# Sliding-window attention, then a dropless mixture of experts, in one program: a pair's gate weights a portion later, the third pair's tasks packed, row stores from SyncE, another order of the first loads, and the index table in two parts

## The chip, the cores and the metric

The kernel runs on one core of one Trainium2 chip. The metric is the device time of one execution, in microseconds; less is better. The core has five engines that run side by side and wait for one another by semaphores: PE (TensorE, matrix products and transposes), DVE (VectorE), ACT (ScalarE), POOL (GpSimd) and SP (SyncE, which here only issues DMA transfers). Each engine works through its own instructions in the order in which the program has them. SP, ACT and POOL issue DMA transfers.

## The reference

```python
# attention: q, k, v are (8, 8, 576, 64): batch, heads, positions, head size
scores = q @ k^T / sqrt(64) + slope[h] * -(|i - j|)     # slope[h] = 2 ** -(h + 1)
scores = where((i - j >= 0) & (i - j < 128), scores, -1e9)
attn   = softmax(scores);  x = attn @ v                 # x as 4608 tokens of 512

# experts: w_gate 512 x 8, w1 8 x 512 x 1024, w2 8 x 1024 x 512
logits = x @ w_gate
e      = argmax(logits);  gate_w = softmax(logits)[e]
y      = relu(x @ w1[e]) @ w2[e]                        # for every token its own expert
out    = gate_w * y
```

Each token goes to one expert, and no token is dropped.

## The kernel before

**Attention.** Two batches make a pair (`bp`, 0 to 3), two heads make a head pair (`hp`, 0 to 3). One pair and one head pair are a unit `u` of 16, and each unit has four portions, so that a counter `i` runs from 0 to 63. Portion `i` does `scores(i + 2)` (PE products into a PSUM tile `sp`, of which there are two; ACT's exponential into `pe`; DVE's multiplication of `pe` by the distance factors `fac`) and then `values` of its own (PE products of `v_sb` and `pe` into a PSUM tile `at`, of which there is one). In the third and fourth portion of a unit, `finish` has ACT copy `at` to `xT` in SBUF, has PE add up the softmax sums in a PSUM tile `m`, and has DVE put these into `sumT`. Because there is one `at`, the second half of a unit can't begin before ACT has copied the first. There are two `m` tiles, shared by all the helpers below.

**A pair's tasks.** When a pair's four units are through, `behind(bp)` queues its routing as a list of portions' worth of work, one entry at the end of each following portion. For each pair: `gate` (PE: logits before scaling; DVE adds the sums), `turn` (PE transposes, ACT copies), `scale_a` and `scale_b` (DVE: divides by the softmax sums, finds the best expert `sel`, and, with ACT's exponential of `ex` in between, the gate weight, which goes to `ext`), `count` (DVE: running counts `pre`), `place` (PE adds the counts of earlier tokens, DVE makes slot numbers), `ones_at` and `enlist` (the token numbers are put into the table `listed` by a product of one-hot matrices), and nine times `row` (PE transposes 128 tokens, ACT copies them to `xs`, POOL adds `ext`, and a DMA writes them to `x_rows` in memory). The fourth pair's tasks lie in the first expert's products (`with_tail`).

**Experts.** `fixed[e]` is a group of 512 tokens of expert e, worked by a Strassen scheme: `strassen1` (first layer) and `strassen2` (second), each of 14 steps of eight matmul rows, with one entry of the list `fill` behind each step. Seven `further` groups of 128 take what is over. A group's tokens come by `gather` (POOL: indirect DMA from `x_rows` by the index table `g_idx`), are scaled by DVE (`to_scale`, tile `xn`), and turned by PE (`to_columns`, tile `xgT`). Expert 0 is taken from the first three pairs alone, so that its `gather` (index by `early_table`) needs only their rows. The indices of all other groups come from `tables`, after `count_all`.

The order of the work on each engine is that of the code: nothing is rearranged by a scheduler (`manual_schedule`).

## Time and profile before

| | us |
|---|---|
| median of three runs | 753.37 (751.31 to 754.02) |
| the profiled execution | 751.79 |
| its span, first to last instruction | 749.8 |
| PE busy | 690.3 (92%) |
| DVE busy | 348.2 (46%) |
| ACT busy | 223.3 (30%) |
| POOL busy | 157.7 (21%) |

Spans and starts are read from the first instruction of the profiled execution. The profiled execution is 2.0 us longer than its span. PE's granted clock is given as a share of full speed: 1.00 is 2.4 GHz and 0.50 is 1.2 GHz; the mean over the span is 0.97. Matmuls are pipelined in the trace, so the start of the next group tells more than the end of one.

### The profile page before, as it was taken

What the parts mean: (1) busy time and instruction counts of PE and PEld (TensorE: products, weight loads), DVE (VectorE), ACT (ScalarE), POOL (GpSimd) and SP (SyncE); (2) the same over time, 40 slices, a digit from 0 to 9 for tenths busy, and PEclk for the clock granted to TensorE, in tenths of its full rate; (3) what the DMA queues carried; (4) which work ended last, traced back from release to release, by engine and by line L of the source; (5) the groups of instructions that cost most, each with busy time, mean ns of one, the idle gap of its engine ahead of it and who ended that gap; (6) DMA issues with size and microseconds to landing.
All of it is one profiled execution on the core that took longest, in us unless ns stands there. A gap on an engine that the chain in (4) does not pass through costs nothing.

```text
span 749.8 us, 14527 instructions
## 1 busy us (share of the span) xinstructions
PE 690.3 (92%) x6204; PEld 574.7 (77%) x6204; DVE 348.2 (46%) x649; ACT 223.3 (30%) x402; POOL 157.7 (21%) x258
## 2 busy tenths in 40 slices
PE   4997986996869979999999999999999999999993
PEld 3876865765748868887888888788788978878891
DVE  2556557557435926551545254254435435433410
ACT  3643553553424312321320231132023123203210
POOL 4310430521502415012102302200230230021020
PEclk9998998998979989999999999999999999999997
DMA  9876674760341746318336732822763382184010
GB/s 255 252 216 218 191 233 123 226 193 30 122 153 72 278 176 231 112 42 295 142 113 205 271 112 73 305 100 109 245 232 113 107 307 90 81 279 143 1 58 7
DMA packets 49756, 122.00 MB, mean 163 GB/s; under 512 B 3648, under 2 KB 14496, under 8 KB 49681
## 3 DMA queue, kind: packets, MB, share of 16 engines
q1 hardware_dynamic: 37856, 85.92, 33.8%
q0 software_dynamic: 10688, 34.16, 13.5%
q8 instruction: 51, 0.84, 0.5%
q10 hardware_dynamic: 1136, 0.88, 0.4%
q14 instruction: 25, 0.20, 0.1%
HBM read 101.79 MB, written 19.96 MB: 162 GB/s over the span
## 4 chain that ended last, share of the span: by engine, by line
issue 53%; POOL 10%; PE 7%; DMA 3%; DVE 1%; ACT 1%; POOLq 0%; ACTq 0%; DVEq 0%
POOL out_dram L1329 5%; POOL xg L1071 5%; DMA xg<-x_rows,g_idx 2%; DMA x_rows<-xs 2%; PE pair0a L1249 1%; PE pair0b L1249 1%; PE m L976 1%; PE m L1088 1%; PE at L767 0%; PE pair2b L1249 0%; PE pair2a L1249 0%; PE pair0a L1306 0%; ACT xs L978 0%; PE m L819 0%; PE m L964 0%
## 5 line engine op out<-in xcount | busy, mean ns | idle before, releaser
L1329 POOL DMA_INDIRECT out_dram<-zo,s_idx x39 | 44.1, 1130 | 385.9 <-DVE zo L1320 284.7
L767 PE MATMUL at<-pe,v_sb 64*64 64x192 f32 (+2 forms) x1408 | 64.7, 301 | 25.2 <-ACT xT L784 20.8
L741 DVE TENSOR_TENSOR pe<-pe,fac 128x768 f32<-128x768 f32 x48 | 46.0, 958 | 61.7 <-ACT pe L738 61.7
L767 PEld LDWEIGHTS at<-pe,v_sb 64*64 64x64 f32 x1408 | 50.0, 144 | 31.8 <-ACT xT L784 23.2
L738 ACT ACTIVATE pe<-sp 128x768 f32<-128x768 f32 x64 | 51.8, 809 | 50.8 <-PE sp L732 49.3
L732 PE MATMUL sp<-q_sb,k_sb 64*64 64x192 f32 (+2 forms) x1152 | 62.0, 335 | 5.3 <-DMA q_sb<-in_qT_dram 5.3
L732 PEld LDWEIGHTS sp<-q_sb,k_sb 64*64 64x64 f32 x1152 | 42.8, 143 | 18.6 <-issue 6.0
L1071 POOL DMA_INDIRECT xg<-x_rows,g_idx x39 | 42.9, 1101 | 22.6 <-issue 11.3
L1089 ACT COPY xgT<-m 128x512 f32<-128x512 f32 x39 | 22.8, 585 | 49.9 <-PE m L1088 49.0
L1088 PE MATMUL m<-ident,xn 128*128 128x128 f32 x156 | 25.8, 292 | 11.4 <-DVE xn L501 11.4
L501 DVE TENSOR_TENSOR xn<-xg 128x512 f32<-128x512 f32 x39 | 26.3, 687 | 21.3 <-DMA xg<-x_rows,g_idx 13.3
L1088 PEld LDWEIGHTS m<-ident,xn 128*128 128x128 f32 x156 | 20.7, 151 | 16.4 <-issue 11.9
L1260 ACT ACTIVATE h<-h 128x512 f32<-128x512 f32 x32 | 20.2, 631 | 36.9 <-DVE h L1259 36.9
L799 PE MATMUL m<-pe,ind 128*32 128x192 f32 (+2 forms) x704 | 31.0, 296 | 0.0
L978 ACT COPY xs<-m 128x512 f32<-128x512 f32 x36 | 20.7, 584 | 33.4 <-PE m L976 23.5
L981 POOL DMA_DIRECT2D x_rows<-xs x40 | 22.2, 556 | 35.9 <-ACT xs L978 19.9
L607 POOL DMA_DIRECT2D v_sb<-in_v_dram x15 | 11.5, 769 | 84.3 <-PE at L767 84.2
L799 PEld LDWEIGHTS m<-pe,ind 128*32 128x32 f32 x704 | 24.3, 114 | 2.7 <-issue 0.4
L979 POOL COPY xs<-ext 128x16 f32<-128x16 f32 x36 | 16.7, 464 | 39.5 <-DVE ext L900 37.7
L976 PE MATMUL m<-ident,xT 128*128 128x128 f32 x144 | 22.7, 286 | 2.4 <-DVE sumT L810 1.0
L746 DVE TENSOR_TENSOR pe<-pe,fac 128x768 f32<-128x768 f32 x16 | 17.4, 1090 | 13.7 <-ACT pe L738 13.7
L976 PEld LDWEIGHTS m<-ident,xT 128*128 128x128 f32 x144 | 16.1, 145 | 7.5 <-issue 2.2
(353 smaller groups left out, 1412.1 us busy)
## 6 DMA issues: line engine op xcount, KB each, us to landing
w<-in_moe_w_dram SPq DMA_DIRECT2D x30, 2048.0 KB, 10.9
k_sb<-in_kT_dram SPq DMA_DIRECT2D x15, 576.0 KB, 5.0
q_sb<-in_qT_dram SPq DMA_DIRECT2D x15, 576.0 KB, 6.3
x_rows<-xs POOLq DMA_DIRECT2D x32, 264.0 KB, 2.5
v_sb<-in_v_dram SPq DMA_DIRECT2D x16, 288.0 KB, 4.0
v_sb<-in_v_dram POOLq DMA_DIRECT2D x15, 288.0 KB, 5.0
x_rows<-xs POOLq DMA_DIRECT2D x8, 132.0 KB, 3.1
xg<-x_rows,g_idx POOLq DMA_INDIRECT x39, 6.6
```

Source lines behind the costliest of these rows:

```text
L501: nc.vector.tensor_tensor(to.rearrange("p (h d) -> p h d", h=H), rows[:, :Dm].rearrange("p (h d) -> p h d", h=H), rows[:, Dm : Dm + H].uns ...
L732: nc.tensor.matmul(sp[c * KB : (c + 1) * KB, r, c0 : c0 + n], lhsT=k_sb[u][hs, c, kb * KB : (kb + 1) * KB], rhs=q_sb[u][hs, c, kb * KB : k ...
L738: nc.scalar.activation(pe[:], sp[:, :, :GC], AF.Exp, scale=SCALE)
L741: nc.vector.tensor_tensor(pe.rearrange("p r (k c) -> p r k c", k=2), pe.rearrange("p r (k c) -> p r k c", k=2), fac[:, h0 : h0 + 2, None, ...
L767: nc.tensor.matmul(acc[r * D : (r + 1) * D, c, lo - q0 : hi - q0], lhsT=v_sb[u][c * KB : (c + 1) * KB, kb, r * D : (r + 1) * D], rhs=pe[c ...
L799: nc.tensor.matmul(sm[32 * j : 32 * j + 32, lo - q0 : hi - q0], lhsT=none[:] if pe is None else ind[:, hp, :], rhs=fac[:, 0, :KB] if pe is ...
L976: nc.tensor.transpose(ps[:, hp * P : (hp + 1) * P], xT[bp][:, hp, t * P : (t + 1) * P], ident[:])
L981: nc.gpsimd.dma_start(x_d[r0 : r0 + n, :], xs[p0 : p0 + n, :])
L1071: nc.gpsimd.indirect_dma_start(out=g["xg"][:, j, :], out_offset=None, in_=src, in_offset=bass.IndirectOffsetOnAxis(ap=g_idx[:, g["c0"] + j ...
L1088: nc.tensor.transpose(tp[:, db * P : (db + 1) * P], xn[:, db * P : (db + 1) * P], ident[:])
L1089: nc.scalar.copy(g["xT"][:, :, j * P : (j + 1) * P], tp.rearrange("p (d q) -> p d q", d=DB))
L1329: ins = nc.gpsimd.indirect_dma_start(out=out[:, :], out_offset=bass.IndirectOffsetOnAxis(ap=s_idx[:, g["c0"] + j : g["c0"] + j + 1], axis= ...
```

## The change

1. **Gate weights later.** `scale_b` ends with `sel`. ACT's exponential and the four DVE operations that make `ext` are a new `scale_c`, one portion later.
2. **A pair's other tasks** move: `count` and `place` go one portion back, the first row lies with `place`, and `enlist` lies one portion later.
3. **The third pair** (`bp == 2`) packs its tasks: all three gates in one entry, all three turns in the next, and so on; ten entries where twelve were, with the first row turned before its gate weight is there (`row_turned`, `row_out`).
4. **The first expert's columns** (`prepare(fixed[0])`) are queued from the second portion of the last unit on; before they came after attention. `prepare` itself is unchanged.
5. **One-hot columns.** POOL's multiplication of `oc` by the token numbers, and DVE's comparison in front of it, become nine DVE operations that do both.
6. **Row stores** are issued by SP; before by POOL.
7. **First loads.** Unit 0's `v` comes in two pieces per half; unit 1's `q` and one half of its `v` are issued by ACT behind the second exponential, and POOL issues no `v` of unit 1.
8. **Tables.** `tables` becomes `table_fixed` (28 columns, straight behind `enlist` of the fourth pair) and `table_further` (7 columns); `count_all` lies behind the second expert's `gather`, and `next_groups` four steps later than before.
9. **The fourth pair** in `strassen1`: gates in one step, turns in the next, three rows turned ahead of their gate weights, two of the eight sums for `w2` moved into `strassen2`.

```diff
@@ first loads
-        load_v(0, 0, nc.sync)
-        load_v(0, 1, nc.scalar)
+        load_v(0, 0, nc.sync, 0, 4)
+        load_v(0, 1, nc.scalar, 0, 4)
+        load_v(0, 0, nc.sync, 4, NK)
+        load_v(0, 1, nc.scalar, 4, NK)
+        load_k(1, 0, S, nc.sync)
-        load_unit(1)
@@ behind the first two scores
+        load_v(1, 0, nc.sync)
+        load_q(1, 0, S, nc.scalar)
+        load_v(1, 1, nc.scalar)
@@ scale_b
-            nc.scalar.activation(ex[:], ex[:], AF.Exp)
+            ex_of[bp] = ex
...
+        def scale_c(bp):
+            ts = slice(bp * TPB, (bp + 1) * TPB)
+            ex, r = ex_of[bp], r_of[bp]
+            nc.scalar.activation(ex[:], ex[:], AF.Exp)
             gw = small.tile([P, TPB], F32, name="gw")
@@ ones_at
-            nc.vector.tensor_tensor(
-                oc[:], K["cols"][:, None, : E * NS].to_broadcast([P, TPB, E * NS]),
-                rc[:, 1, :].unsqueeze(2).to_broadcast([P, TPB, E * NS]), op=ALU.is_equal,
-            )
-            nc.gpsimd.tensor_tensor(
-                oc[:], oc[:],
-                K["tok"][:, bp * TPB : (bp + 1) * TPB].unsqueeze(2).to_broadcast([P, TPB, E * NS]), op=ALU.mult,
-            )
+            for t in range(TPB):
+                nc.vector.tensor_scalar(
+                    oc[:, t, :], K["cols"][:, : E * NS], scalar1=rc[:, 1, t : t + 1],
+                    scalar2=K["tok"][:, bp * TPB + t : bp * TPB + t + 1], op0=ALU.is_equal, op1=ALU.mult,
+                )
@@ row
-                nc.gpsimd.dma_start(x_d[r0 : r0 + n, :], xs[p0 : p0 + n, :])
+                nc.sync.dma_start(x_d[r0 : r0 + n, :], xs[p0 : p0 + n, :])
@@ behind
             if bp == 2:
-                return first[:6] + [first[6] + rs[0:1], first[7] + rs[1:2], ones + rs[2:4], put_in + rs[4:6],
-                                    [early_table] + rs[6:9], [lambda: gather(fixed[0], x_d[: 3 * 2 * S, :])]]
-            return first + [ones + rs[0:1], rs[1:2], put_in + rs[2:3], rs[3:4], rs[4:5], rs[5:6], rs[6:7], rs[7:9]]
+                return [g3, t3, a, b + [lambda: row_turned(bp, 0)], c + n + [lambda: row_out(bp, 0)], p + rs[1:3], o + rs[3:5], e + rs[5:7], [early_table] + rs[7:9],
+                        [lambda: gather(fixed[0], x_d[: 3 * 2 * S, :])]]
+            return [g3[0:1], g3[1:2], g3[2:] + t3[0:1], t3[1:], a, b, c, n, p + rs[0:1], o + rs[1:2], rs[2:3],
+                    e + rs[3:4], rs[4:5], rs[5:6], rs[6:7], rs[7:9]]
@@ the loop over portions
+            if u == len(units) - 1 and g == 1:
+                tasks.extend(t for _, t in prepare(fixed[0]))
@@ with_tail
-                [lambda: gate(bp, 0), lambda: gate(bp, 1)], [lambda: gate(bp, 2), lambda: turn(bp, 0)],
-                [lambda: turn(bp, 1), lambda: turn(bp, 2)], [lambda: scale_a(bp)], [], [lambda: scale_b(bp)],
-                w[0] + rs[0:2], [lambda: count(bp)] + w[1] + rs[2:4], [lambda: place(bp)] + rs[4:6],
-                [lambda: ones_at(bp)] + rs[6:7], w[2] + w[3] + rs[7:8], [lambda: enlist(bp)] + w[4] + rs[8:9],
-                [count_all] + w[5], [tables] + w[6] + w[7],
+                [lambda k=k: gate(bp, k) for k in range(3)], [lambda k=k: turn(bp, k) for k in range(3)], a, early[0:2], b,
+                early[2:3] + w[0], c + n + w[1] + [lambda t=t: row_out(bp, t) for t in range(3)], rs[3:5], p + rs[5:6], o + rs[6:7], w[2] + w[3] + rs[7:9], e + w[4],
+                [table_fixed], w[5],
@@ second layer of the first expert
-                fill.append((g, [next_groups, lambda: gather(fixed[1], x_d[:, :])]))
-                fill.extend([(g, [])] * 3)
+                fill.append((g, [lambda: gather(fixed[1], x_d[:, :]), self_late[0]]))
+                fill.append((g, [self_late[1], count_all]))
+                fill.append((g, [table_further]))
+                fill.append((g, [next_groups]))
                 fill.extend(prepare(fixed[1], close=True))
```

**ACT in unit 5**, which holds the tasks of the first pair. `pe<-sp` is the exponential of a portion's scores, `xT<-at` the copy that frees `at`, `ex<-ex` the exponential for the gate weight. Before:

```order
L738 ACTIVATE pe<-sp 128x768 x2
L883 ACTIVATE ex<-ex 128x72
L738 ACTIVATE pe<-sp 128x768
L784 COPY xT<-at 128x2x320
L738 ACTIVATE pe<-sp 128x768
L784 COPY xT<-at 128x2x192
```

Now, at the same place:

```order
L742 ACTIVATE pe<-sp 128x768 x3
L788 COPY xT<-at 128x2x320
L901 ACTIVATE ex<-ex 128x72
L742 ACTIVATE pe<-sp 128x768
L788 COPY xT<-at 128x2x192
```

`ex` stood ahead of a portion's exponential and of the copy out of `at`; now both are ahead of it. The same holds in units 9 and 13.

**PE at the passage from unit 5 to unit 6.** `m<-pe,ind` ends `finish` of unit 5, `m<-pre,lt_strict` is the product of `place`, `sp<-q_sb,k_sb` are scores, `at<-pe,v_sb` values, `m<-ident,xT` turns a row. Before:

```order
L799 MATMUL m<-pe,ind 32x64 x2
L916 MATMUL m<-pre,lt_strict 128x8
L732 MATMUL sp<-q_sb,k_sb 64x192 x8
L767 MATMUL at<-pe,v_sb 64x192 x8
L976 MATMUL m<-ident,xT 128x128 x4
```

Now:

```order
L803 MATMUL m<-pe,ind 32x64 x2
L736 MATMUL sp<-q_sb,k_sb 64x192 x8
L771 MATMUL at<-pe,v_sb 64x192 x8
L922 MATMUL m<-pre,lt_strict 128x8
L981 MATMUL m<-ident,xT 128x128 x4
```

`place` stands one portion later, and the row behind it is the one that was there before.

**DVE from the fourth pair's `enlist` on**, at the end of `strassen1`: `listed` is the table, `w2s`, `hs` and `h` are Strassen sums, `n` begins `count_all`, `tok_f` begins `table_fixed`, `g_idx` are the indices for `gather`. Before:

```order
L971 TENSOR_TENSOR listed<-m,listed 128x48
L537 TENSOR_TENSOR w2s<-w_3019 128x512
L529 TENSOR_TENSOR hs<-h 128x512
L530 TENSOR_TENSOR hs<-hs,h 128x512
L531 TENSOR_TENSOR h<-h 128x2x256
L1017 COPY n<-m 128x12
L1018 TENSOR_TENSOR n<-n,hole 128x1
```

Now:

```order
L974 TENSOR_TENSOR listed<-m,listed 128x48
L537 TENSOR_TENSOR w2s<-w_3061 128x512
L529 TENSOR_TENSOR hs<-h 128x512
L530 TENSOR_TENSOR hs<-hs,h 128x512
L531 TENSOR_TENSOR h<-h 128x2x256
L1067 COPY tok_f<-listed 128x28
L1006 TENSOR_SCALAR tb_3369<-tok_f 128x28
L1007 TENSOR_SCALAR ta_3368<-tok_f 128x28
L1008 TENSOR_SCALAR ta_3368<-ta_3368 128x28
L1009 CAST g_idx<-ta_3368 128x28
```

The indices of the fixed groups follow the table at once; before, all of `count_all`, six Strassen sums and the further groups' tokens stood between.

## Rows read from the trace of the kernel before

**Rows 1.** Busy time by stretch: us, busy time and instructions of each engine, granted clock, DMA.

```profile
0.00:20.50 20.50, 11.02 (x138) 8.34 (x142) 6.30 (x9) 6.78 (x10) 7.90 (x37) 1.00 0.96 259
...
64.90:69.90 5.00, 0.00 (x0) 0.00 (x0) 4.66 (x14) 1.54 (x3) 0.00 (x0) 0.86 1.03 410
69.90:75.40 5.50, 5.46 (x89) 4.50 (x89) 2.70 (x6) 1.46 (x3) 0.73 (x1) 0.51 0.25 99
...
169.70:174.70 5.00, 0.00 (x0) 0.00 (x0) 4.69 (x15) 1.54 (x3) 0.00 (x0) 0.96 0.00 0
174.70:181.00 6.30, 6.27 (x86) 4.77 (x90) 2.65 (x5) 2.04 (x4) 1.64 (x3) 0.50 0.12 43
205.10:216.10 11.00, 3.89 (x21) 2.94 (x18) 3.19 (x5) 1.76 (x3) 2.05 (x2) 0.65 0.81 278
216.10:219.10 3.00, 3.00 (x9) 2.13 (x7) 2.28 (x4) 0.58 (x1) 0.00 (x0) 0.57 0.00 0
263.60:267.90 4.30, 0.05 (x2) 0.07 (x2) 0.69 (x1) 0.37 (x1) 1.44 (x2) 0.83 1.02 405
267.90:273.40 5.50, 5.50 (x18) 4.65 (x19) 1.54 (x3) 0.74 (x2) 0.00 (x0) 0.51 0.49 192
```

**Rows 2.** Waits of PE: line and tile, releaser, us in total, times, longest.

```profile
PE at L767 <- ACT xT L784: 20.8, 13, 5.7
PE m L1088 <- DVE xn L501: 11.4, 5, 4.3
...
PE m L964 <- POOL oc L949: 1.5, 1, 1.5
```

**Rows 3.** Timeline of ACT and DVE in units 5 and 6: start, duration, [idle time before].

```profile
68.34 0.26 ACT L883 ACTIVATE ex<-ex 128x72 f32<-128x72 f32 x1 [4.79 <-DVE ex L882]
...
69.20 0.68 ACT L784 COPY xT<-at 128x640 f32<-128x640 f32 x1
69.24 0.22 DVE L897 TENSOR_REDUCE gw<-ex 128x9 f32<-128x72 f32 x1
...
70.17 0.95 DVE L741 TENSOR_TENSOR pe<-pe,fac 128x768 f32<-128x768 f32 x1
71.04 0.48 DVE L810 TENSOR_TENSOR sumT<-m,sumT 128x320 f32<-128x320 f32 x1
71.44 0.30 DVE L907 TENSOR_TENSOR_SCAN pre<-keep,sel 128x72 f32<-128x72 f32 x1
```

**Rows 4.** Timeline of PE at place and at the first row behind it.

```profile
75.40 0.39 PE L916 MATMUL m<-pre,lt_strict 128*128 128x8 f32 x2
...
77.18 0.66 PE L976 MATMUL m<-ident,xT 128*128 128x128 f32 x4
```

**Rows 5.** Timeline from the first gather to the last scaled tokens of expert 0 (four gathers).

```profile
202.67 1.12 POOL L1071 DMA_INDIRECT xg<-x_rows,g_idx  x1 [3.04 <-DMA x_rows<-xs]
...
206.21 0.69 DVE L501 TENSOR_TENSOR xn<-xg 128x512 f32<-128x512 f32 x1 [0.59 <-DMA xg<-x_rows,g_idx]
...
214.20 0.69 DVE L501 TENSOR_TENSOR xn<-xg 128x512 f32<-128x512 f32 x1 [0.79 <-DMA xg<-x_rows,g_idx]
```

**Rows 6.** Timeline from the fourth pair's table to the tokens of expert 1.

```profile
248.92 0.21 DVE L971 TENSOR_TENSOR listed<-m,listed 128x48 f32<-128x48 f32 x1 [0.66 <-PE m L964]
...
260.01 1.55 POOL L1071 DMA_INDIRECT xg<-x_rows,g_idx  x1 [8.28 <-DVE tb L998]
...
267.02 0.69 DVE L501 TENSOR_TENSOR xn<-xg 128x512 f32<-128x512 f32 x1 [5.10 <-DMA xg<-x_rows,g_idx]
```

**Rows 7.** Timeline of ACT and PE in the first 20 us.

```profile
8.44 0.81 ACT L738 ACTIVATE pe<-sp 128x768 f32<-128x768 f32 x1 [1.73 <-PE sp L732]
...
14.77 1.22 PE L767 MATMUL at<-pe,v_sb 64*64 64x192 f32 x10 [3.54 <-DMA v_sb<-in_v_dram]
...
18.41 1.21 PE L732 MATMUL sp<-q_sb,k_sb 64*64 64x192 f32 x11
```

**Rows 8.** DMA issues: size of each, median us from issue to landing.

```profile
q_sb<-in_qT_dram SPq DMA_DIRECT2D x15, 576.0 KB, 6.3
```

More of the change, by code (lines that the diff above doesn't have):

```diff
@@ L976, in row, with row_out @@
                 nc.tensor.transpose(ps[:, hp * P : (hp + 1) * P], xT[bp][:, hp, t * P : (t + 1) * P], ident[:])
-            xs = rows.tile([P, RW], F32, name="xs")
+            xs = xs_of[bp, t] = rows.tile([P, RW], F32, name="xs")
             nc.scalar.copy(xs[:, :Dm], ps[:])
+        def row_out(bp, t):
+            xs = xs_of.pop((bp, t))
             nc.gpsimd.tensor_copy(xs[:, Dm:], K["ext"][:, bp * TPB + t, :])
             for p0, n, r0 in placed(bp, t):
-                nc.gpsimd.dma_start(x_d[r0 : r0 + n, :], xs[p0 : p0 + n, :])
+                nc.sync.dma_start(x_d[r0 : r0 + n, :], xs[p0 : p0 + n, :])
+        def row(bp, t):
+            row_turned(bp, t)
+            row_out(bp, t)
         NC = E * NJ + XU
@@ L1051, in count_all, with table_fixed, table_further @@
             nc.vector.tensor_copy(xe[:], xf[:])
-        def tables():
-            pick = K["pick"]
+        def table_fixed():
+            tok = K["tok_f"] = rte.tile([P, (E - 1) * NJ], F32, name="tok_f")
+            nc.vector.tensor_copy(tok.rearrange("p (e j) -> p e j", e=E - 1), listed[:, 1:, :NJ])
+            index(slice(NJ, E * NJ), tok[:], "1")
+        def table_further():
             px = rte.tile([P, XU, E * NF], F32, name="px")
@@ L1107, in later, with prepare @@
             return [lambda k=k: run(k) for k in range(n)]
-        def behind(bp):
-            first = [
-                [lambda: gate(bp, 0)], [lambda: gate(bp, 1)], [lambda: gate(bp, 2), lambda: turn(bp, 0)],
-                [lambda: turn(bp, 1), lambda: turn(bp, 2)], [lambda: scale_a(bp)], [lambda: scale_b(bp)],
-                [lambda: count(bp)], [lambda: place(bp)],
-            ]
+        def prepare(g, close=False):
+            n = g["n"]
+            cols = [lambda j=j: to_columns(g, j) for j in range(n)]
+            scales = [lambda j=j: to_scale(g, j) for j in range(n)]
+            todo = [[scales[0]]] + [[cols[j], scales[j + 1]] for j in range(n - 1)] + [[cols[n - 1]]]
+            if n == NJ:
+                sums = later(lambda: x_sums(g), 4)
+                if "ws" not in g:
+                    sums += later(lambda: w1_sums(g), 8)
+                todo[-1].append(sums.pop(0))
+                todo += [[f] for f in sums] if not close else [sums[k : k + 2] for k in range(0, len(sums), 2)]
+            return [(g, t) for t in todo]
+        def behind(bp):
+            g3 = [lambda k=k: gate(bp, k) for k in range(3)]
+            t3 = [lambda k=k: turn(bp, k) for k in range(3)]
             rs = [lambda t=t: row(bp, t) for t in range(TPB)]
-            ones, put_in = [lambda: ones_at(bp)], [lambda: enlist(bp)]
+            a, b, c, n, p, o, e = (
+                [lambda f=f: f(bp)] for f in (scale_a, scale_b, scale_c, count, place, ones_at, enlist)
+            )
             if bp == 2:
-                return first[:6] + [first[6] + rs[0:1], first[7] + rs[1:2], ones + rs[2:4], put_in + rs[4:6],
-                                    [early_table] + rs[6:9], [lambda: gather(fixed[0], x_d[: 3 * 2 * S, :])]]
-            return first + [ones + rs[0:1], rs[1:2], put_in + rs[2:3], rs[3:4], rs[4:5], rs[5:6], rs[6:7], rs[7:9]]
+                return [g3, t3, a, b + [lambda: row_turned(bp, 0)], c + n + [lambda: row_out(bp, 0)], p + rs[1:3], o + rs[3:5], e + rs[5:7], [early_table] + rs[7:9],
+                        [lambda: gather(fixed[0], x_d[: 3 * 2 * S, :])]]
+            return [g3[0:1], g3[1:2], g3[2:] + t3[0:1], t3[1:], a, b, c, n, p + rs[0:1], o + rs[1:2], rs[2:3],
+                    e + rs[3:4], rs[4:5], rs[5:6], rs[6:7], rs[7:9]]
         tasks = []
```

44 lines of the change are left out of this document (18 added, 26 removed).

## The prediction

> **What bounds the kernel now.** The share of busy time comes first: PE works 92% of the span and no other engine reaches half, so only time in which PE stands still, or runs at half clock, can be won. The chain that sets the end is PE's own order of work. The list of what PE waits for [rows 2] gives the two places to look: its products into `at` wait 20.8 us for ACT's copy `xT`, in 13 waits, and its column turns 11.4 us for DVE's `xn`, in 5. The busy time by stretch [rows 1] shows where these lie and what they cost besides. At 64.9 and again at 169.7 PE does nothing for 5.0 us, while DVE is busy for 4.7 of them; at 263.6 it does nothing for 4.3. Behind each of the three follow 5.5 to 6.3 us in which the granted clock is 0.50 or 0.51 with PE full, so each stop costs about half of that stretch again, 2.7 to 3.2 us. From 205.1 to 216.1, between attention and the first expert, PE has 3.9 us of work in 11.
>
> The timeline of the first stop [rows 3] tells its cause. ACT is idle for 4.8 us in front of `ex`, waiting for DVE. The copy `xT` that frees `at` is behind `ex` on ACT (69.20), so PE waits for the routing of a pair that it has no need of yet. Unit 9 has the longest such wait, 5.7 us [rows 2].
>
> I add up against the profiled execution, 751.79, which is 1.6 us below the median of the three runs (753.37). A difference of under 0.5%, some 3.8 us, can hardly be told from no change here.
>
> **The start: −2.2.** PE waits 3.5 us for unit 0's `v_sb`, until 14.77 [rows 7]. With `v` in pieces and unit 1's loads behind, values can start when DVE has finished `pe`, up to 4.5 us earlier. But unit 1's `q` is now issued by ACT behind its second exponential, which ends at 8.44 + 0.81 = 9.25 [rows 7]; with the 6.3 us that a `q` takes to land [rows 8] it is there at about 15.6, and with the issue at 16.2. PE did unit 1's scores at 18.4 before. So 2.2 are left. The bounds are 0 (the loads only change places in a full queue) and 4.5 (q comes before it is wanted).
>
> A row shows that bandwidth is the limit in this stretch: DMA is at 0.96 and 259 GB/s over the first 20.5 us [rows 1]. The Trainium skill (page "DMA: Bandwidth & Descriptors", section "Issuing engines are not separate DMA queues") says that transfers of all issuing engines run on the same 16 DMA engines, and that issuing from several saves only the time to issue. By that only the order and number of bytes count, unit 1's `q` would be there before PE asks, and the start would give 4.5 instead of 2.2: 724 in all. No run so far shows which.
>
> **The first pair: −3.8.** With `ex` one portion later, the copy `xT` no longer waits and PE goes on into the next portion. What is late next is `place`, which needs `pre` from DVE. DVE's chain is only moved: from 69.24 come a portion's `pe` (70.17 to 71.04, 0.87) and `sumT` (0.40), the gate weight (69.24 to 70.17, 0.93), the next portion's `pe` and `sumT` (1.27), and the count (0.30) [rows 3]. 69.24 + 0.87 + 0.40 + 0.93 + 1.27 + 0.30 = 73.0. Before, `place` stood at 75.40 and the first row behind it at 77.18, with a portion's scores and values between them [rows 4]. These now lie ahead of `place`, so the row follows `place` (0.39) at 73.4: 77.2 − 73.4 = 3.8 earlier. This counts the half clock after the old stop as not paid; what the new waits do to the clock is a term of its own below.
>
> **The second pair: −2.4.** It is the same chain, but two Strassen sums of `w1` fall to DVE inside it. An operation of one such tensor, 128x512, takes 0.69 [rows 5]: 3.8 − 1.4 = 2.4.
>
> **The third pair and the first gather: −16.2.** Before, attention ended at 205.1 [rows 1]. Taken away are the stop of 5.0, half of the 6.3 us at half clock (3.15) [rows 1], and the 1.5 us that PE waited for POOL's `oc` [rows 2]. Added is the wait of `place` for `pre`: 5.0 less a portion's scores and values that PE now does meanwhile (1.8, [rows 4]), so 3.2. Two of the four column turns now lie inside attention, each of four transposes like a row's (0.66, [rows 4]): 1.3. 205.1 − 5.0 − 3.15 − 1.5 + 3.2 + 1.3 = 199.95. The other two turns follow, 1.3, and the first expert can start at 201.25, if its tokens are there. Before it started at 216.1, and its first 3.0 us ran at clock 0.57 [rows 1], which cost 1.3. 216.1 − 201.25 + 1.3 = 16.2.
>
> Are the tokens there? The first gather was issued at 202.67 after a wait of 3.0 for the last store [rows 5]. The packed list ends two portions earlier; 64 portions fill the time to 205.1, about 3.0 us each, so 6.0. The portions in front come 5.2 earlier (205.1 − 199.95), and 202.67 − 6.0 − 5.2 = 191.5; if the stores from SP, which has nothing else to do there, take half of the 3.0 away, it is 190. Three more gathers follow at 1.3 us each (1.1 to 1.55, [rows 5, 6]). The first landed 3.5 us after its issue (202.67 to 206.21), while the last came 11.5 behind the first, beside a load of weights [rows 5]. So the last tokens are there between 190 + 3.9 + 3.5 = 197.4 and 191.5 + 11.5 = 203.0, and are wanted at 200.6. I take the first, since the weights' load begins at attention's end as before; the other end costs 2.4.
>
> **The fourth pair's tasks: 0.** They are the same instructions in other steps of `strassen1`, where nothing but `oc` showed as a wait in attention; bounds −0.9 and +1.5 (one wait like that for `oc`, [rows 2], either way).
>
> **The second gather: −6.3.** `listed` was done at 248.92, the gather went out at 260.01, 8.3 us of it POOL's wait for DVE's tables [rows 6]. Now four DVE sums (at most 0.69 each) and five small operations stand between: about 3.3. The gather goes out at 252.2 and its tokens land 7.0 later (260.01 to 267.02, [rows 6]), at 259.2. DVE has the same work in front of `xn` as before, and was through with it at 267.02 − 5.10 = 261.9 [rows 6]; since it is now handed out one entry per step of `strassen2`, behind the gather, I put the first `xn` later, at 264.3. PE came to wait at 263.6 [rows 1]. So 0.7 of 4.3 stays, and the half clock behind it (5.5 us at 0.51, 2.7) goes: 3.6 + 2.7 = 6.3. Ends: 1.3 (tokens late by 5) and 7.0.
>
> **The row stores, `oc`, the late `next_groups`: 0.** SP has long idle stretches; its loads for attention are two units ahead. A store waits on SP for its row, and the next `k`, `q` and `v` stand behind it. Three portions of 3.0 us and the 6.3 us of a `q` [rows 8] still leave some 9 us of two units' 24. Nine small DVE operations replace one on DVE and one on POOL. If the cover is gone it costs what a `q` takes, 6 us in each pair, and the upper end has one of them.
>
> **The clock: +5.4.** The new waits are real stops. In the first pair 73.0 − 64.9 = 8.1 us hold the products that took 5.5 at half clock [rows 1], so 2.8, and a portion's scores and values, 1.8 [rows 4]; the other 3.5 PE stands still, in two parts, for `pe` and then for `pre`. In the third it is 3.2 in one. The three long stops, 4.3 to 5.0, all had 5.5 us and more at half clock behind them [rows 1], which cost 2.7. The wait for `v_sb` of 3.5 [rows 7] lies in a stretch with clock 1.00 [rows 1]. The new waits lie near that one, so neither case is excluded. I take a fall in two pairs of three: 2 × 2.7 = 5.4, with 0 and 8.1 as ends. The Trainium skill (page "TensorE: Matmul & The Clock Gate", section "HAM oscillation — how this bites in real kernels") tells of a kernel that falls to the low clock at every one of its repeated waits and pays each time. By that all three fall, the term is 8.1 and the time 729; the row of the wait for `v_sb` speaks for fewer.
>
> **Sum.** 2.2 + 3.8 + 2.4 + 16.2 + 0 + 6.3 − 5.4 = 25.5, and 751.8 − 25.5 = 726.3. I predict 726.
>
> **Rivals.**
> *The clock stays full and the start gives all it can.* Then the 5.4 are not paid and the start gives 2.3 more: 718.6; with one of the two, 721 or 724. For it: the clock 1.00 around the wait for `v_sb`. Against it: two waits in a row.
> *The stop changes its name.* PE waits for `pre` where it waited for `xT`, the clock falls in all three pairs (+2.7), and DVE's chain is some 2 us longer in two of them: 733. For it: DVE was busy 4.7 of the 5.0 us [rows 1], and none of its work is removed. Against it: the 1.8 us of products that now lie ahead.
> *The first gather is late.* The tokens come as the last ones did before, 203.0, and a gap of over 2.4 us with a new fall of 2.7 follows; with stores of SP that land 3 us later it is 8 in all: 734. For it: the gather waited 3.0 for a store before. Against it: DMA is empty at 174.7 to 181 (0.12).
> *Slower: SP in order.* A store that waits for its row keeps unit u+2's `k`, `q` and `v` back, and PE waits for loads in every pair. It decides when a store is held for more than the lead of 9 us; to undo the sum it must cost 8.5 us in each of three pairs (752 in all; 757 at 10). Against it: a row is turned and copied in about 2 us once `place` is through.
> *No effect.* PE would have to be as late as before for another reason, at 205.1 above all: 750 to 754.
>
> **How the numbers follow.** Forecast (721 to 731) 0.50; better (716 to 721) 0.18; the stop changes its name (731 to 735) 0.15; first gather late (731 to 738) 0.12; SP 0.03; no effect 0.02. The best end takes 0 for the clock and 4.5 for the start, and 0.9 of the fourth pair and 0.7 of the second gather on top: 717. The worst takes 0 for the start (+2.2), three falls (+2.7), the late gather of expert 1 (+5.0) and the tail (+1.5), 737.7; 738. Between these is 0.9 of the chance, and I keep them, since one late transfer alone reaches 732. Faster by over 0.5% has 0.95, within it 0.02, slower 0.03.
>
> **What would show it.** In units 5, 9 and 13 ACT's `ex` stands behind `xT`, and PE's wait for `xT` falls from 20.8 to under 8 us in all; in its place PE waits 2 to 3 us for `pre` at `place`. The granted clock behind those three places tells the clock's term. The first gather goes out near 190, the first expert begins near 201. The second gather follows `listed` by some 3 us, and the wait for `xn` of 4.3 falls under 1. Values begin near 10.3 and unit 1's scores near 16. The prediction is wrong if PE stops over 5 us anywhere before 270, or if a load of `k` or `q` ends one of its waits.

## The result, and the profile after

The changed kernel takes 730.0 us (median of four runs, 728.99 to 730.51), the kernel before 752.5 (751.31 to 754.02): a ratio of 0.9698, interval 0.9674 to 0.9722. The forecast was 726: 721 to 731 with a chance of one half, 717 and 738 as ends. The profiled execution took 728.99, with a span of 727.2, 22.6 less than before. One of the four executions of the first experiment below took 1419.2 us at full clock, and its median leaves that one out; nothing kept here tells why.

What PE waits for now, as in [rows 2]:

```profile
PE sp L736 <- DMA q_sb<-in_qT_dram: 13.9, 3, 8.7
PE m L922 <- DVE pre L913: 6.7, 3, 3.0
PE at L771 <- ACT xT L788: 5.7, 12, 0.5
PE m L967 <- ACT xs L983: 1.4, 1, 1.4
...
PE m L1104 <- DVE xn L501: 0.6, 1, 0.6
```

The two waits that led the list are gone: 20.8 for `xT` is 5.7 in many short ones, 11.4 for `xn` is 0.6. Two stand in their place: `pre`, foreseen, and an 8.7 us wait for a `q`, not foreseen. The busy time by stretch, as in [rows 1], shows what these do to the clock. The engines stand in the order PE, PE's weight loads, DVE, ACT, POOL, and the last three numbers are the granted clock, the DMA engines' busy share, and GB/s:

```profile
15.00:21.00 6.00, 0.00 (x0) 0.03 (x1) 0.00 (x0) 0.00 (x0) 0.00 (x0) 0.50 1.07 273
21.00:25.50 4.50, 4.50 (x80) 3.83 (x84) 1.45 (x2) 1.39 (x2) 0.00 (x0) 0.57 0.63 218
72.00:78.00 6.00, 3.99 (x90) 3.04 (x94) 5.65 (x17) 2.62 (x5) 1.86 (x4) 1.00 0.94 271
120.00:126.00 6.00, 3.46 (x84) 2.52 (x76) 5.72 (x18) 2.31 (x5) 2.18 (x4) 1.00 0.47 122
126.00:131.00 5.00, 4.93 (x60) 3.88 (x64) 3.87 (x14) 1.66 (x3) 0.43 (x1) 0.66 0.14 55
167.00:170.00 3.00, 0.26 (x3) 0.29 (x3) 2.83 (x10) 0.70 (x2) 0.40 (x1) 1.00 0.06 14
170.00:175.00 5.00, 5.00 (x79) 4.25 (x83) 3.66 (x14) 2.47 (x4) 1.05 (x4) 0.67 0.44 165
198.50:201.10 2.60, 1.95 (x26) 1.47 (x17) 1.62 (x3) 1.21 (x4) 0.00 (x0) 1.00 0.26 67
232.20:239.00 6.80, 6.79 (x27) 6.07 (x28) 3.94 (x12) 1.08 (x2) 0.00 (x0) 0.57 0.81 261
```

At the start PE is idle with DMA full, and then runs 4.5 us at 0.57. Behind the first pair's waits the clock stays at 1.00, behind the second's and third's it falls for a part of 5 us. The gap of 11 us between attention and the first expert is now 2.6 us, most of it column turns. At 232 there is a new fall.

The places where the prediction set a time, in the order of the program (timeline rows of PE, DVE and POOL):

```profile
21.00 1.56 PE L736 MATMUL sp<-q_sb,k_sb 64*64 64x192 f32 x16 [8.67 <-DMA q_sb<-in_qT_dram]
76.47 0.36 PE L922 MATMUL m<-pre,lt_strict 128*128 128x8 f32 x2 [1.75 <-DVE pre L913]
76.69 0.63 PE L981 MATMUL m<-ident,xT 128*128 128x128 f32 x4
190.04 1.07 POOL L1087 DMA_INDIRECT xg<-x_rows,g_idx  x1 [5.47 <-DVE sumT L814]
201.10 1.89 PE L1270 MATMUL pair0a<-xgT,w 128*128 128x256 f32 x8
235.54 0.21 DVE L974 TENSOR_TENSOR listed<-m,listed 128x48 f32<-128x48 f32 x1 [2.72 <-PE m L967]
239.37 0.97 POOL L1087 DMA_INDIRECT xg<-x_rows,g_idx  x1 [11.11 <-DVE tb L1010]
250.48 1.28 DVE L501 TENSOR_TENSOR xn<-xg 128x512 f32<-128x512 f32 x2
```

To see which stage gave what, one instruction at each border is set against the same one before. Before (timeline; the end of unit 4, the end of unit 7, the first copy of unit 11, the first product of `strassen1`, of `strassen2`, the first and last scatter of results):

```profile
58.75 0.47 ACT L784 COPY xT<-at 128x384 f32<-128x384 f32 x1
98.19 0.28 ACT L786 COPY xT<-at 128x128 f32<-128x128 f32 x1
146.43 0.69 ACT L784 COPY xT<-at 128x640 f32<-128x640 f32 x1
215.92 2.34 PE L1249 MATMUL pair0a<-xgT,w 128*128 128x256 f32 x5
253.08 1.24 PE L1306 MATMUL pair1a<-w,h 128*128 128x256 f32 x5
282.05 1.22 POOL L1329 DMA_INDIRECT out_dram<-zo,s_idx  x1 [16.71 <-DVE zo L1320]
738.20 0.98 POOL L1329 DMA_INDIRECT out_dram<-zo,s_idx  x1 [13.24 <-ACT zo L1367]
```

Now (the fourth border, 201.10, stands above):

```profile
62.09 0.47 ACT L788 COPY xT<-at 128x384 f32<-128x384 f32 x1
97.79 0.28 ACT L790 COPY xT<-at 128x128 f32<-128x128 f32 x1
144.94 0.69 ACT L788 COPY xT<-at 128x640 f32<-128x640 f32 x1
241.11 1.89 PE L1327 MATMUL pair1a<-w,h 128*128 128x256 f32 x8
263.43 1.24 POOL L1350 DMA_INDIRECT out_dram<-zo,s_idx  x1 [19.02 <-DVE zo L1341]
719.60 0.98 POOL L1350 DMA_INDIRECT out_dram<-zo,s_idx  x1 [13.24 <-ACT zo L1388]
```

| stage | offset at its end | stage gave | predicted |
|---|---|---|---|
| start, to unit 4 | +3.3 | +3.3 | −2.2 |
| first pair's tasks | −0.4 | −3.7 | −3.8 |
| second pair's tasks, with a fall of the clock | −1.5 | −1.1 | −2.4 + 2.7 |
| third pair and passage, with a fall | −14.8 | −13.3 | −16.2 + 2.7 |
| `strassen1` with the fourth pair | −12.0 | +2.8 | 0 |
| second gather | −18.6 | −6.7 | −6.3 |
| all later groups | −18.6 | 0 | 0 |
| from the last scatter to the end of the span | −22.6 | −4.0 | 0 |

A plus means that time was lost. Before, a loss of 1.3 us by the low clock at 216.1 fell behind the fourth border; counted with the third pair, as the prediction did, that stage gave −14.6 and `strassen1` +4.1.

### The profile page after: what moved, and what is told of

Read it like the earlier page. It is cut to its first block, busy times and chain, and to the rows that moved or that the text cites. A ratio compares the mean times of both kernels' runs of the same rounds, so it can differ in the third digit from the quotient of the medians.

```text
span 727.2 us, 14595 instructions
## 1 busy us (share of the span) xinstructions
PE 683.9 (94%) x6204; PEld 570.4 (78%) x6204; DVE 351.2 (48%) x687; ACT 222.5 (31%) x402; POOL 122.0 (17%) x213
## 4 chain that ended last, share of the span: by engine, by line
PE 49%; issue 23%; POOL 4%; DVE 3%; ACT 1%; POOLq 0%; ACTq 0%; DVEq 0%
PE pair0a L1327 3%; PE pair0b L1327 3%; PE pair0b L1270 3%; PE pair2b L1270 3%; PE pair0a L1270 3%; PE pair1a L1327 3%; PE pair1b L1327 3%; PE pair2a L1270 3%; PE pair1b L1270 2%; PE pair2a L1327 2%; PE pair2b L1327 2%; PE pair1a L1270 2%; POOL out_dram L1350 2%; PE pair2a L1382 2%; PE sp L736 2%
## 5 line engine op out<-in xcount | busy, mean ns | idle before, releaser
L745 DVE TENSOR_TENSOR pe<-pe,fac 128x768 f32<-128x768 f32 x48 | 45.9, 956 | 59.4 <-ACT pe L742 59.3
L736 PE MATMUL sp<-q_sb,k_sb 64*64 64x192 f32 (+2 forms) x1152 | 59.4, 328 | 13.9 <-DMA q_sb<-in_qT_dram 13.9
L771 PE MATMUL at<-pe,v_sb 64*64 64x192 f32 (+2 forms) x1408 | 60.8, 290 | 7.3 <-ACT xT L788 5.7
L736 PEld LDWEIGHTS sp<-q_sb,k_sb 64*64 64x64 f32 x1152 | 41.1, 140 | 25.6 <-issue 14.5
L771 PEld LDWEIGHTS at<-pe,v_sb 64*64 64x64 f32 x1408 | 47.4, 139 | 13.2 <-ACT xT L788 7.7
L1105 ACT COPY xgT<-m 128x512 f32<-128x512 f32 x39 | 22.9, 586 | 36.4 <-PE m L1104 35.4
L987 POOL COPY xs<-ext 128x16 f32<-128x16 f32 x36 | 11.0, 318 | 87.2 <-DMA x_rows<-xs 50.3
L1104 PE MATMUL m<-ident,xn 128*128 128x128 f32 x156 | 23.6, 274 | 0.6 <-DVE xn L501 0.6
L1104 PEld LDWEIGHTS m<-ident,xn 128*128 128x128 f32 x156 | 19.2, 141 | 4.9 <-PE m L1104 0.9
L1382 PE MATMUL pair2a<-w,h 128*128 128x512 f32 x48 | 21.1, 592 | 0.0
L750 DVE TENSOR_TENSOR pe<-pe,fac 128x768 f32<-128x768 f32 x16 | 15.3, 956 | 10.7 <-ACT pe L742 10.7
```

What stands on the lines that cost most here:

```text
L736: nc.tensor.matmul(sp[c * KB : (c + 1) * KB, r, c0 : c0 + n], lhsT=k_sb[u][hs, c, kb * KB : (kb + 1) * KB], rhs=q_sb[u][hs, c, kb * KB : k ...
L745: nc.vector.tensor_tensor(pe.rearrange("p r (k c) -> p r k c", k=2), pe.rearrange("p r (k c) -> p r k c", k=2), fac[:, h0 : h0 + 2, None, ...
L771: nc.tensor.matmul(acc[r * D : (r + 1) * D, c, lo - q0 : hi - q0], lhsT=v_sb[u][c * KB : (c + 1) * KB, kb, r * D : (r + 1) * D], rhs=pe[c ...
L1104: nc.tensor.transpose(tp[:, db * P : (db + 1) * P], xn[:, db * P : (db + 1) * P], ident[:])
L1382: nc.tensor.matmul(ps[:], lhsT=g["h"][:, fb, :], rhs=g["w2"][:, fb, :], start=(fb == 0), stop=(fb == FB - 1),)
```

## Experiments

Each is the changed kernel with one edit, until the ninth. Ratios are to the kernel before on the same chip; the changed kernel's is 0.9698. "More" and "less" are differences to that ratio, times the 752 us of the kernel before. Of the first eight, only the fifth and the seventh have an interval clear of the changed kernel's 0.9674 to 0.9722, and the third's just touches it; the times of the other five can't be told from the changed kernel's, so there the rows decide and not the time.

**1 and 2. The start.** Unit 1's loads as before; then as changed, but with `q` ahead:

```diff
@@ experiment 1
-        load_v(0, 0, nc.sync, 0, 4)
-        load_v(0, 1, nc.scalar, 0, 4)
...
-        load_k(1, 0, S, nc.sync)
+        load_v(0, 0, nc.sync)
+        load_v(0, 1, nc.scalar)
+        load_unit(1)
@@ experiment 2
         load_k(1, 0, S, nc.sync)
+        load_q(1, 0, S, nc.sync)
...
-        load_q(1, 0, S, nc.scalar)
```

> The changed kernel with the first loads as before (unit 0's v in two halves, all of unit 1's loads behind them from SP and POOL). Theory A: the new order of loads put unit 1's q behind k, q and v of unit 2 in a full queue, so PE got it at 21.0 instead of 18.4 and ran at half clock after an 8.7 us stop; all later work stands 3.1 to 3.3 us later for it. Then this kernel has PE's unit 1 scores at 18.4 again, no clock fall there, and takes 726.7 (3.3 less than the changed kernel's 730.0). Rival B: the queue is full either way and the start only looks different, later work catches up: 729 to 731.

> The changed kernel, but unit 1's q is issued by SP right behind unit 1's k instead of by ACT behind the second exponential. Theory A (the place in the queue decides): five loads with 2.9 MB lie ahead of its end at some 260 GB/s, 11.4 us, so it is there at 13 to 14, PE does unit 1's scores at about 14 and the clock stays full: 7 earlier plus 2 of half clock, less what v of unit 1, now the last, holds back (0 to 4): 721 to 726. Rival B: 729 to 731.

Measured: 728.71, ratio 0.9669 (0.9634 to 0.9705), and 727.74, 0.9683 (0.9652 to 0.9714). The long wait went in both. With `q` ahead, unit 1's scores start at 13.09, and 10 us later its `v` is late. With the old loads a stop without a named releaser comes at 31.8 (PE, one row of each; the first is the second experiment's):

```profile
13.09 0.88 PE L737 MATMUL sp<-q_sb,k_sb 64*64 64x192 f32 x16 [1.72 <-DMA q_sb<-in_qT_dram]
23.14 1.22 PE L772 MATMUL at<-pe,v_sb 64*64 64x192 f32 x10 [2.71 <-DMA v_sb<-in_v_dram]
```

```profile
31.80 1.07 PE L801 MATMUL m<-pe,ind 128*32 128x192 f32 x12 [4.13 <-issue]
```

So theory A holds for the place in the queue. The gain, though, is 1 to 2 us by the ratios, within their intervals, instead of 3.3 and 4 to 9, so that rival B is not excluded by the time: while DMA is full, what is moved ahead pushes something else back.

**3. The gate weight back** into the portion of the choice.

```diff
-            return [g3[0:1], g3[1:2], g3[2:] + t3[0:1], t3[1:], a, b, c, n, p + rs[0:1]
+            return [g3[0:1], g3[1:2], g3[2:] + t3[0:1], t3[1:], a, b + c, [], n, p + rs[0:1]
```

In the third pair it is `b + c`, then `n`, in the same way.

> The changed kernel, with the gate weight (the exponential ex and its DVE operations) in the same portion as the choice of the expert again; nothing else is moved. Theory A: this part alone took the stop of PE at the copy out of at away. Then the 5.0 us stops of units 5, 9 and 13 come back, the waits for pre (1.8, 2.0, 3.0) and the other new ones of unit 9 (1.9) go, and the clock falls in all three: +3.2 +2.7, +1.8, +2.1, so about 740. Rival C: the stop went because the tasks lie in other portions, and the gate weight's place is worth little: under 733.

Measured: 733.28, ratio 0.9743 (0.9716 to 0.9771), 3.4 more. PE at the three places:

```profile
73.51 1.24 PE L771 MATMUL at<-pe,v_sb 64*64 64x64 f32 x20 [5.06 <-ACT xT L788]
126.28 1.24 PE L771 MATMUL at<-pe,v_sb 64*64 64x64 f32 x20 [5.66 <-ACT xT L788]
176.02 0.57 PE L922 MATMUL m<-pre,lt_strict 128*128 128x8 f32 x2 [2.18 <-DVE pre L913]
```

The stops of units 5 and 9 come back as theory A has it, in unit 13 none: there something else in the change had removed it, most likely the packed tasks, which no run undoes by themselves. Theory A's 740 was too high, for that and because the changed kernel has falls of the clock already. The time lies just outside C's bound, and the rows decide for A in two pairs and for C in the third.

**4. The count ahead** of the gate weight.

```diff
-            return [g3[0:1], g3[1:2], g3[2:] + t3[0:1], t3[1:], a, b, c, n, p + rs[0:1]
+            return [g3[0:1], g3[1:2], g3[2:] + t3[0:1], t3[1:], a, b + n, c, [], p + rs[0:1]
```

In the third pair it is `b + n`, then `c`.

> The changed kernel, with the count (pre) straight behind the choice of the expert in the same portion, ahead of the gate weight; place stands where it did. Theory D: place waits for pre only because pre stands behind two portions' worth of other DVE work. Then the waits of 1.8, 2.0 and 3.0 for pre go, and with them the falls of the clock in units 9 and 13 (about 2 each): 730.0 - 6.8 - 4 = 719. Rival E: DVE itself is too late (it has no less work), PE waits the same time for the next thing that DVE makes, pe or sumT, and the clock falls all the same: 728 to 731.

Measured: 728.41, ratio 0.9683 (0.9657 to 0.971). Rival E is right. `cn`, which `place` makes of its product, is what the slot numbers start from:

```profile
74.01 0.88 PE L771 MATMUL at<-pe,v_sb 64*64 64x192 f32 x16 [1.61 <-DVE pe L745]
76.34 0.92 PE L981 MATMUL m<-ident,xT 128*128 128x128 f32 x4 [1.14 <-DVE sumT L814]
169.34 0.36 PE L922 MATMUL m<-pre,lt_strict 128*128 128x8 f32 x2 [1.44 <-DVE pre L913]
171.91 0.92 PE L981 MATMUL m<-ident,xT 128*128 128x128 f32 x4 [1.50 <-DVE cn L926]
```

PE waits 1.44 + 1.50 = 2.94 in unit 13, where it waited 2.98 for `pre`. DVE is late as a whole there (in the changed kernel it had 2.83 us of work in the 3.0 us from 167.0); the order of its work only chooses the name of the wait. The clock falls behind the waits in all three units, in unit 5 too, where the changed kernel's had stayed full.

**5 to 8.** Row stores on POOL; the first expert's columns behind attention; one whole index table, with `count_all`, two sums for `w2` and `next_groups` ahead of the second gather again; the fourth pair's last two rows in two steps:

```diff
@@ experiment 5
-                nc.sync.dma_start(x_d[r0 : r0 + n, :], xs[p0 : p0 + n, :])
+                nc.gpsimd.dma_start(x_d[r0 : r0 + n, :], xs[p0 : p0 + n, :])
@@ experiment 6
-            if u == len(units) - 1 and g == 1:
-                tasks.extend(t for _, t in prepare(fixed[0]))
...
@@ experiment 7
-                [table_fixed], w[5],
+                [count_all] + w[5], [table_fixed, table_further] + w[6] + w[7],
...
@@ experiment 8
-                w[2] + w[3] + rs[7:9], e + w[4],
+                w[2] + w[3] + rs[7:8], e + w[4] + rs[8:9],
```

> The changed kernel with the row stores issued by POOL again. From the last scatter's issue to the end of the span it is 11.5 us before the change (738.2 to 749.8) and 7.5 to 8.0 in the changed kernel and in the first four experiments, all with stores from SP. Theory F: fewer transfers in POOL's software queue make the end shorter; then this kernel ends 11 to 12 us after its last scatter, and with a first gather that goes out up to 3 us later it takes 733 to 737. Rival G: the end has its 4 us from another part; then it stays at 7.5 to 8 and the kernel takes 729 to 733.

Measured: 734.25, ratio 0.9768 (0.9745 to 0.979), 5.3 more; theory F. The last scatter is issued at 719.31 and the span ends at 730.5, 11.2 later, where it is 7.6 in the changed kernel and 7.2 to 8.0 in every other experiment:

```profile
719.31 0.98 POOL L1350 DMA_INDIRECT out_dram<-zo,s_idx  x1 [13.24 <-ACT zo L1388]
```

So stores from SP instead of POOL save 3.6 us at the very end, 480 us after the last of them. The trace shows where: at the program's end, POOL has three DRAIN instructions, at the line of the block around the whole kernel, one of them long (durations in ns: smallest, median, longest). In the kernel before, in this one, and in the changed one:

```profile
L1482 POOLq DRAIN  x3: 46/103/6113, 742.9 to 749.6; - x3
L1507 POOLq DRAIN  x3: 46/103/5787, 723.9 to 730.3; - x3
L1507 POOLq DRAIN  x3: 46/103/2765, 723.6 to 727.0; - x3
```

That is 3.02 of the 3.6 us; the DRAIN also starts 0.6 later behind the scatter (4.6 us for 4.0). Its length goes with what POOL has issued in the whole kernel: 2765 ns in the changed kernel and in all experiments with the same transfers on POOL, 3092 in the first, where POOL issues one load of `v` more, and 2438 in the twelfth, with one less. What the DRAIN does in that time is not shown.

> The changed kernel with the first expert's columns behind attention again, as one block. Theory H: the third pair's packed tasks alone bring the tokens in time, and the early columns only save PE's wait on DVE's scaling and ACT's copies at the passage: then the first expert starts 3 to 6 us later than 201.1, 733 to 736. Rival I: most of the 13 us gained at the passage is due to the early columns: 738 to 742.

Measured: 730.43, ratio 0.9723 (0.9696 to 0.9751), 1.9 more: neither, H is the nearer. From the last copy of attention to the first product of `strassen1` it is 4.2 us (199.99 to 204.15), in the changed kernel 2.7 (198.45 to 201.10). The early columns are worth 1.5 us at this place. The rest of what the passage gained goes with the gather's earlier issue: 8.8 us ahead of the end of attention's products (190.04 to 198.80), where it was 2.4 before (202.67 to 205.1). No run undoes that by itself.

> The changed kernel with the index table whole again: count_all and the further groups' indices ahead of the second gather. Theory J: the second gather goes out 8 to 11 us behind the listed table again, PE waits about 4 us for the tokens of expert 1 and runs 5 us at half clock: 6 to 7 more, 736 to 737. Rival K: since the fourth pair's tasks lie otherwise now, only the wait of 4 comes back, or less: 731 to 734.

Measured: 735.21, ratio 0.9773 (0.9747 to 0.9798), 5.6 more. The gather goes out 10.6 us behind the table (238.13 to 248.73), and PE's wait is back, with a fall of the clock (0.66 from 256 to 261):

```profile
256.28 1.12 PE L1104 MATMUL m<-ident,xn 128*128 128x128 f32 x4 [3.86 <-DVE xn L501]
```

Theory J, at a smaller fall than before (1.6 us lost for 2.7).

> The changed kernel with the fourth pair's last two rows in two steps instead of one (the eighth where both stood, the ninth with the table). Theory L: PE's wait of 1.41 us in front of the table's product, in all five kernels with this part so far, comes from two rows that hold both m tiles while ACT's copies stand behind a relu that waits for DVE; with one row a step it goes, and with it the fall of the clock that followed it in the changed kernel and in the first experiment, but not in the other three: 726 to 729. Rival M: DVE's nine operations for oc are what is late, and PE waits as long for the next thing: 729 to 731.

Measured: 728.03, ratio 0.9681 (0.9659 to 0.9703). The wait for `xs` is not among PE's waits any more (0.4 for DVE's `orow` is left), and from the first product of `strassen1` to that of `strassen2` it is 35.4 us; theory L:

```profile
204.25 1.25 PE L1270 MATMUL pair0a<-xgT,w 128*128 128x256 f32 x5
239.65 1.24 PE L1327 MATMUL pair1a<-w,h 128*128 128x256 f32 x5
```

The changed kernel needs 40.0 for it. But the fourth experiment, with the same wait of 1.41, needs 36.7, since there the clock stayed full behind it (busy time by stretch):

```profile
233.50:240.00 6.50, 6.45 (x39) 5.94 (x40) 4.70 (x15) 2.31 (x4) 0.38 (x1) 1.00 0.82 242
```

So of the changed kernel's 40.0 the wait is 1.3 and the fall that followed it in this execution is 3.3.

**9 to 12. A better version.** The ninth has all of unit 1's loads from SP at once, the rows of the eighth, the choice in a portion of its own with `place` later in the first two pairs, the third pair's count ahead of its gate weight, and three DVE operations (`low`, `bad`) moved behind the rows. The tenth moves the third pair's gate weight to `place`. The eleventh moves the Strassen sums of `w1` to units 10 and 11. The twelfth has unit 2's loads issued by ACT behind the fourth exponential.

```diff
@@ experiment 9
-        load_k(1, 0, S, nc.sync)
+        load_unit(1)
...
-            return [g3[0:1], g3[1:2], g3[2:] + t3[0:1], t3[1:], a, b, c, n, p + rs[0:1]
+            return [g3[0:2], g3[2:] + t3[0:1], t3[1:], a, b1, b2, n + c, [], p + rs[0:1]
@@ experiment 10, third pair
-            a, b + n + [lambda: row_turned(bp, 0)], c + [lambda: row_out(bp, 0)], p + rs[1:3], o + rs[3:5]
+            a, b + n + [lambda: row_turned(bp, 0)], [], p + c + [lambda: row_out(bp, 0)] + rs[1:2], o + rs[2:5]
@@ experiment 11
-            if 8 <= u < 12 and g % 2 == 1:
+            if 10 <= u < 12:
@@ experiment 12
...
+            if i == 1:
+                load_unit(2, nc.scalar)
```

> A version made of what the runs pointed to: all of unit 1's loads from SP ahead of unit 2's; the fourth pair's last two rows in two steps; in the first two pairs the gates packed into one portion less, the choice of the expert in a portion of its own, the count ahead of the gate weight and place one portion later than that; the three checking operations (low, bad) of each pair moved behind its rows; in the third pair count ahead of the gate weight. Theory A and D together: start 6 to 8 less, tail 1.4, units 5 and 9 two waits (3.0 each) and a fall of the clock (1.5 to 2) less, third pair 1 less: 730 - 7 - 1.4 - 8 - 1 = 713, at most 718. Rival E (DVE has no less work, the waits only change their names, and the clock falls as before): 720 to 722.

> The same, but in the third pair the gate weight stands with place, one portion later, and the rows are handed out behind it. If DVE's gate weight and the portion's other DVE work between sel and place is what PE still waits for there (3.0 us in the fourth experiment, as pre 1.4 and cn 1.5), 1.5 to 3 of it go and the first gather goes out no later than 1 us behind: 1.5 to 4 less than the ninth experiment. If the rows come too late for the gather, PE waits for xn at the passage and it is 1 to 4 more.

> The tenth experiment's kernel, with the eight Strassen sums of w1, which lay in units 8 to 11 (every second portion), all in units 10 and 11. Theory D2: DVE's work beside the second pair's routing is what PE still waits for in unit 9 (1.6 us and a half-clock stretch of some 7 us in the tenth experiment); without the sums there the wait goes under 0.7 and the clock stays full: 2.5 to 4 less than the tenth, 718 to 719. Rival: the sums stand in portions with slack, and the wait stays, 721 to 722, or it moves to units 10 and 11.

> The same, and unit 2's loads are issued by ACT behind the fourth exponential (about 12.5) instead of by SP at once, so that unit 1's have the queue alone. The ninth and tenth have two losses at the start: 1.1 to 1.9 us for unit 1's q at 13.5, and a stop of 3.5 us at 28 in the middle of PE's products for the softmax sums, for which the trace names no releaser, with DMA at 1.0 and more from 18 to 30. Theory N: both come from transfers that are not needed yet; then q is there by 12.5, the stop at 28 goes or shrinks, and the fall of the clock behind it goes: 3 to 7 less than the eleventh. Rival: unit 2 comes late instead (PE waits for k, q or v between 20 and 30), or the stop stays, since the bytes in flight at 28 are those of units 3 and 4: same as the eleventh within 1.

Measured, with ratios: 721.79, 0.9641 (0.9601 to 0.9681); 721.70, 0.9629 (0.9594 to 0.9663); 720.16, 0.9609 (0.9583 to 0.9635); 718.45, 0.9606 (0.957 to 0.9642). By the ratios they take 4.3, 5.2, 6.7 and 6.9 us less than the changed kernel; the kernel before was faster on these chips too (749.6 and 749.1), so the times as they stand flatter them. The ninth's 721.79 is rival E's number, but by the ratio it gained less than either theory gave it (8 to 10, or 12 to 17). `place` waits no more in the first two pairs, but at 27.7 PE stops for 3.6 us in a group it has begun, with no releaser named (below), and in unit 13 it is `cn` again (1.50). In the tenth the wait for `cn` is gone, and with it the fall of the clock behind it, without a difference in time that is clear of the intervals. The eleventh is 1.5 lower by its ratio, within the intervals; the wait in unit 9 stayed (1.41 for 1.62), as its rival said, though the clock stayed full behind it this time. In the twelfth the stop at 27.7 is gone; unit 2's `q` is waited for instead, as its rival said:

```profile
24.02 0.88 PE L736 MATMUL sp<-q_sb,k_sb 64*64 64x192 f32 x16 [2.70 <-DMA q_sb<-in_qT_dram]
```

Its profiled execution has the shortest span of all, 713.3, with one fall of the clock left; but its four times run from 715.0 to 721.6, and by the ratio it is 0.2 less than the eleventh (the rival's "same within 1"). Both are faster than the changed kernel: their intervals lie below its own.

## Why the prediction was right, and where it was off

**The total: right, in part by luck.** 22.6 us came for the 25.5 of the sum. The start missed by 5.5 and the fourth pair by 2.8; the 4.0 us from the row stores, put at nothing, make up for almost half of that, and the second pair's 1.4 for some more. Without the stores' 4.0 the changed kernel would take 734, outside 721 to 731, though inside the ends. And by the prediction's own sign it is wrong in one place: PE was not to stop over 5 us before 270, and no load of `q` was to end one of its waits; at 21.0 both happened, in the one stop of 8.67 us.

**First pair: right, number and mechanism.** `ex` stands behind the copy, PE's wait for `xT` went, `place` waits for `pre`. The chain on DVE gave `place` at 73.0; with the 3.3 of the start that is 76.3, and it was 76.47. −3.7 for −3.8. The third experiment shows that the gate's place is the cause in units 5 and 9. The second pair gave 2.8 for 2.4, less a fall of the clock that cost 1.7.

**Clock: right in number, not in size.** Two falls were taken, and two came, in units 9 and 13, but each cost 1.7 us (5 us at 0.66 and 0.67) where 2.7 was taken: 3.4 for 5.4. Two more were not in the term, at the start (1.9) and at 232 (3.3, see the fourth pair), so that all four cost 8.6. What decides whether a fall comes is not shown: behind waits of 1.24 and 1.76 us in unit 5 the clock stayed full in the first experiment's profile and fell in the fifth's. The Trainium skill (page "TensorE: Matmul & The Clock Gate", section "HAM oscillation — how this bites in real kernels") tells of a fall at each repeated wait; the traces agree that short waits can be paid twice, but not that each is.

**Third pair and passage: right, cause in part argued.** Gather forecast at 190, issued at 190.04; first expert at 201.25, started at 201.10. The agreement is closer than it should be: the prediction set these two times without the gain of the earlier stages (1.5 us in the end), and without that gain they would have been 191.5 and 202.6. The stage gave 14.6 for 13.5 (16.2 less a fall of 2.7, which cost 1.7). From the end of attention's products to the first expert it is 2.3 us for 10.8. The sixth experiment shows what the prediction had lumped: the early columns are the small part of it. The packed tasks and the one-hot columns on DVE are left with the rest; no run takes them back.

**Second gather: right.** 3.8 behind `listed` for 3.3, and −6.7 for −6.3. Of the wait of 4.3 nothing is left, where 0.7 was taken: PE turns expert 1's columns at 251.92 without a stop, and the one wait for `xn` still in the list, 0.65, is at 200.03, for expert 0. The seventh experiment undoes it.

**Start: wrong, by 5.5.** `v` in pieces did what it was to do: the wait of 3.5 for it is gone, and values begin at 9.36. The step that failed: "with the 6.3 us that a `q` takes to land [rows 8] it is there at about 15.6". It was issued at 8.40, 0.9 earlier than forecast, and PE had it at 21.0, 12.6 later. The 6.3 is a median of loads in attention, most of them not urgent and not in a full queue; here unit 2's `k` (issued by SP at 6.15), `q` (8.40) and `v` were ahead of it or beside it. The Trainium skill's rule (page "DMA: Bandwidth & Descriptors", section "Issuing engines are not separate DMA queues") agrees with that: issued by ACT, the `q` still shared the DMA engines with SP's loads. In the second experiment SP issued it at 4.53, 3.9 earlier and ahead of unit 2's loads, and it was there by 13.09, after 8.6. The 18.4 that its sum starts from is not the first of unit 1's scores, either: they began at 17.89 before. What failed in the 4.5 that the prediction drew from the rule is the count of bytes, which left out those of unit 2.

**Fourth pair: wrong, by 2.8 to 4, outside its bound of 1.5.** "The same instructions in other steps" overlooked what stands in one step. Two rows take both `m` tiles; ACT copies them out behind a relu, which waits for DVE's `h`, which stands behind nine operations for `oc` (2.02 us) and `orow` (1.35):

```profile
227.14 2.02 DVE L952 TENSOR_SCALAR oc<-cols,rc,tok 128x48 f32<-128x48 f32 x9
...
230.34 0.68 DVE L1280 TENSOR_TENSOR h<-pair2a,u 128x512 f32<-128x512 f32 x1
...
231.06 0.63 ACT L1281 ACTIVATE h<-h 128x512 f32<-128x512 f32 x1 [2.69 <-DVE h L1280]
231.59 1.05 ACT L983 COPY xs<-m 128x512 f32<-128x512 f32 x2
232.21 2.01 PE L967 MATMUL m<-oc,orow 128*128 128x48 f32 x12 [1.41 <-ACT xs L983]
```

The eighth experiment takes the wait away by the rows alone. The wait by itself lies inside the bound: with it and a full clock the fourth experiment needs 36.7 for `strassen1`, 0.8 more than the 35.9 of before without its low clock. It is the fall behind it, 3.3, that goes beyond.

**Row stores: costed at 0, worth 3.6 to 4.0.** SP's order cost nothing, as said: loads do stand behind stores (a `k` goes out at 89.27, behind four stores from 78.0 on), but PE waits for no load after 21.0. The gain at the end was not foreseen, since nothing ahead of the last scatter is a part of it; the fifth experiment shows it, and the DRAIN where it lies. (The rival on SP has a slip: 10 us in each of three pairs give 756, not 757.)

## What to carry to other kernels

A transfer's landing time is that of its queue at that moment: take what lies ahead of it in bytes, by all engines, and not a median over the kernel. When a stop of PE comes from one engine that is late as a whole, moving one operation gives only what other work fits into the stop; after that the wait changes its name until that engine has less to do. Short stops of PE can cost twice or three times their length by the clock, but not each does, and the profile of one kernel shows a fall that the next one's lacks behind the same stop: price them as a range, and compare stages by a border instruction in several profiles. A sum that comes out right is not yet a mechanism that is right: set every stage against its own term.
